# Value products in six-unit blocks, three banks for first scores, and a new order of scores and maxima's transposes in a block-attention kernel

## The chip, the cores and the metric

The kernel runs on one core of one Trainium2 chip. Its time is device microseconds of that core; lower is better. The kernel before takes 678.67 us (median of 3 runs, 678.55 to 678.76). A core has TensorE (PE in the profile, with its weight loads as PEld), VectorE (DVE), ScalarE (ACT), GpSimd (POOL), and SyncE (SP), whose queue issues all DMAs here. [...]

## The reference

One transformer block with adaptive layer norms: sliding-window attention (16 heads of 28, window of 256 keys), then a dense layer with Mish. S = 2048 positions, D = 448, F = 1792.

```python
def _A_ref(x, wqkv, wo):
    H = 16; Dh = D // H; W = 256
    qkv = (x @ wqkv).reshape(B, S, 3, H, Dh).transpose(2, 0, 3, 1, 4)
    q, k, v = qkv[0], qkv[1], qkv[2]
    scores = jnp.einsum("bhqd,bhkd->bhqk", q, k) * (Dh ** -0.5)
    mask = (idx[:, None] - idx[None, :] >= 0) & (idx[:, None] - idx[None, :] < W)
    p = _softmax(jnp.where(mask, scores, -1e9))
    return einsum("bhqk,bhkd->bhqd", p, v).transpose(0, 2, 1, 3).reshape(B, S, D) @ wo

h = _layernorm(x) * (1 + ca) + sa
x = x + ga * _A_ref(h, A_wqkv, A_wo)
h = _layernorm(x) * (1 + cb) + sb
x = x + gb * (mish(h @ B_w1 + B_b1) @ B_w2)
```

(sa, ca, ga, sb, cb and gb are six rows of silu(c) @ w_mod.)

## The kernel before, in words

**Stages.** A start (to about 37 us) loads x and the weights and makes the first projections. Attention runs from there to about 376 us, with the projections of the next row group, the output projection of the last one and the loading of the dense layer's weights between its steps. Then the dense layer runs to the end, matmuls on `z` and `acc`.

**Tiling of attention.** The 2048 rows are four groups g of 512 (`GT`). A *slot* i is one head in one row group; there are 64 (`NS`), and four consecutive slots make a *quad* q of 12 units. For each slot the keys are those of its 512 rows and of the 256 before them, six tiles jj of 128. Their allowed pairs of (key tile, query tiles) are three blocks b of 512 columns (`BLOCKS`): 128 + 384, 256 + 256, and 384 + 128. In the first row group, whose keys begin with the group, the blocks have 384, 256 and 384 + 128 columns. A *unit* u is one block of one slot: `unit(u)` gives slot 4q + r % 4 and block r // 4, with r = u % 12. So units 0 to 3 of a quad are block 0 of its four heads, 4 to 7 block 1, 8 to 11 block 2.

**The steps.** The softmax needs each row's maximum ahead of its exponentials, so scores are computed twice:

- `A(i, t)` (first scores): one matmul of a query tile t with the 384 keys that it can see, into a PSUM bank `sA` (L687). VectorE adds the mask and takes the maximum over the keys into `mx` (L689, which appears as two rows, the reduction `junk` and the read of its accumulator). A quad's 16 first scores belong to the quad *after* the one that is being exponentiated. After the last score of a pair of slots, `M1` splits the 8 maxima into two parts `ms` on VectorE (L700, L701).
- `M2(pr)` transposes a pair's `ms` on TensorE (L705, `mt`), VectorE copies it to `mr` (L707), and a DMA writes it into two rows of the pair's query tile (`q<-mr`), so that the second scores come out with the maximum subtracted.
- `L(i)` loads a slot's queries and keys by two DMAs (`q<-scr`, `k<-scr`); `load_slot` calls it at r = 8, 11, 2 and 4.
- `B(u)` (second scores): the mask through small matmuls (L759) or through a copy by ScalarE (`seeds`, L739), then the score matmuls (L731) into one of two banks `sB`, then the exponential on ScalarE into `P` (L734), a ring of seven buffers.
- `PV(w)` (value products): for four units, the matmuls of `V` with `P` into the bank `pv` (L769), in fp32, which shows as two matmul rows each. Each head's 28 value columns and a column of ones are padded to 32, and head a of the quad writes partitions 32a to 32a + 31. A program matmul is made for each width and head, the narrower width first.
- `EV(q)` copies the finished bank to SBUF on ScalarE (L775), `E(q)` transposes it on TensorE in four pieces into a bank (L780, `et`), and `E2(q)` reads that bank on VectorE: the reciprocal of the sums (L788) and the scaling (L790, `on`).

**Order.** Every engine works its instructions off in program order. The loop over u writes them: a step of `pipe` (evacuations that lag behind their matmuls); then, where u - 5 is a multiple of 4, `PV` of the four units that are complete, and `EV` after a quad's third; then `B(u)`; then the first scores that are due at r; `M2` at r = 7 and r = 11; `load_slot`; `E` at r = 3 and `E2` at r = 4 for the quad before; then projections as `RATE[g]` allows (`step(g)`) and a step of the side work (`side_step`), which holds a VectorE piece back where two first scores are due; last the second score of this r. Score n of 16 is due at r = 1 + n * 10 // 16: two each at r = 1, 2, 4, 6, 7 and 9, one at 3, 5, 8 and 10.

**Banks of PSUM.** In attention: `sA` two, `sB` two, `mm` two (projections), `pv` one, and `tr` one, which `M2` and `E` share. A bank that is asked for again is waited for until its last reader has read it. In the last four slots (i >= 60) every other first score takes an `mm` bank. At the start `tr` also holds one of the three first projections (`first`).

Of the kernel before, what the change touches and what calls it, by code (L numbers as in the profile page):

```python
# [20 lines left out]
NQ, NK, NV = 8, 8, 10  # L21
# [30 lines left out]
def adaln_block(ctx: ExitStack, tc: tile.TileContext, x, wqkv, wo, w1, b1, w2, c, w_mod, out):  # L52
    nc = tc.nc
    PE, ACT, DVE, POOL = nc.tensor, nc.scalar, nc.vector, nc.gpsimd
# [3 lines left out]
    def dma(o, i):  # L58
        nc.sync.dma_start(o, i)
# [25 lines left out]
    def bank(tag, bufs, name):  # L85
        return PS[0].tile([128, 512], F32, name=name, tag=tag, bufs=bufs)
# [22 lines left out]
    two = wqkv[:, 128:1152].rearrange("r (a n) -> r a n", n=512)[:, :, 0:256]  # L109
# [41 lines left out]
    V = [(vp if j < 6 else vq).tile([128, H, 32], F32, name=f"v{j}") for j in range(NV)]  # L151
# [53 lines left out]
    def passes(xh, xl, wh, wl):  # L205
        r = []
        for ci in range(3):
            r += [(xh[:, ci], wh[:, ci]), (xh[:, ci], wl[:, ci]), (xl[:, ci], wh[:, ci])]
        return r + [(xh[:, 3], wh[:, 3]), (xl[:, 3], wh[:, 3])]
# [7 lines left out]
    def dup(x):  # L217
        POOL.tensor_copy(x[:, D:512], x[:, 384:448])
# [92 lines left out]
    def drain(*gs):  # L311
        for g in gs:
            for _ in g:
                pipe.step()
# [16 lines left out]
    def flush():  # L331
        while later:
            later.pop(0)()
# [45 lines left out]
    def qk_passes(g, m):  # L379
        ms = slice(QPOS[m], QPOS[m] + 128)  # L380
        return passes(*HT[g], wq3[:, :, ms], wql[:, :, ms])
# [56 lines left out]
    def wq_lo(part, ci, eng):  # L438
        c = slice(*QCOLS[part])
        split_lo(wqs[ci][:, c], wq3[:, ci, c], wql[:, min(ci, 2), c], ci, eng)  # L440
# [27 lines left out]
    sums(0, (2, 3), DVE)  # L468
    for t in range(4):
        dup(XS[0][t])  # L470
    pm = [bank("sA", 2, f"mc{h}") for h in range(2)]
    trs = [bank(*((f"sB{ci}", 1) if ci < 2 else ("mm", 2)), f"tr0{ci}") for ci in range(4)]
    hh, hl = HT[0] = [mid.tile([128, 4, GT], F32R, name=f"h{n}0", tag="on", bufs=2) for n in "hl"]
    warm = bank("pv", 1, "warm")
# [22 lines left out]
    for ci in (2, 3):  # L497
        wq_hi(0, ci)
        wq_lo(0, ci, POOL)
    first = [(m, bank(tag, b, f"qk0_{m}"), qk_passes(0, m)) for m, tag, b in ((0, "pv", 1), (3, "tr", 1), (4, "sA", 2))]  # L500
    def passes0(cs, half):
        for m, p, ps in first:
            for ci in cs:
                for n in range(3 * ci, min(3 * ci + 3, 11)):
                    if (n == 10 or n < 9 and n % 3 == 2) == half:
                        PE.matmul(p, ps[n][1], ps[n][0], start=(n == 0), stop=(n == 10))  # L506
# [159 lines left out]
    NS = NG * H  # L666
    NU = 3 * NS
    mx, Pt, pvb, et, O4 = {}, {}, {}, {}, {}
# [11 lines left out]
    def A(i, t):  # L680
        g, h = divmod(i, H)
        q, k = Q3[i % NQ], K3[i % NK]
        if i % 2 == 0 and t == 0:
            mx[i // 2] = att.tile([128, 2, 4], F32, name=f"mx{i}", tag="mx", bufs=2)
        c0 = max(256 - 128 * t, 0) if g == 0 else 0
        p = bank("mm" if i >= 60 and t % 2 else "sA", 2, f"sA{i}_{t}")
        PE.matmul(p[:, c0:384], q[0:84, t * 128:(t + 1) * 128], k[0:84, t * 128 + c0:t * 128 + 384],  # L687
                  start=True, stop=True)
        DVE.tensor_tensor_reduce(out=junk[:, c0:384], in0=p[:, c0:384], in1=mask[:, c0:384], scale=1.0,  # L689
                                 scalar=-3.0e38, op0=ALU.add, op1=ALU.max,  # L690
                                 accum_out=mx[i // 2][:, i % 2, t:t + 1])
        if i % 2 and t == 3:
            M1(i // 2)
# [3 lines left out]
    def M1(pr):  # L697
        m = ms[pr] = att.tile([128, 2, 8], F32R, name=f"ms{pr}", tag="ms", bufs=2)
        x = mx[pr].rearrange("p a t -> p (a t)")
        DVE.tensor_copy(m[:, 0], x)  # L700
        DVE.tensor_tensor(m[:, 1], x, m[:, 0].bitcast(F32), op=ALU.subtract)  # L701

    def M2(pr):
        p = bank("tr", 1, f"mt{pr}")
        PE.transpose(p[0:16, 0:128], ms[pr].rearrange("p i x -> p (i x)").bitcast(F32), ident)  # L705
        r = att.tile([16, 128], F32, name=f"mr{pr}", tag="mr", bufs=2)
        DVE.tensor_copy(r, p[0:16, 0:128])  # L707
        dma(Q2[pr % (NQ // 2)][84:86].bitcast(F32).rearrange("i a (t n) -> i (a t) n", t=4), r)

    def units(g, b):  # L710
        return [x for x in BLOCKS[b] if g > 0 or x[0] >= 2]

    def by_width(blocks):
        return sorted(blocks, key=lambda x: x[2] - x[1])
# [44 lines left out]
            PE.matmul(p[:, c:c + n], identr, strip[:, m:m + n], start=(i == 0), stop=False, skip_group_check=True)  # L759

    def PV(w):
        q, b = divmod(w, 3)
        g, h = divmod(4 * q, H)
        if b == 0:
            pvb[q] = bank("pv", 1, f"pv{q}")
        for n, (jj, t0, t1, c) in enumerate(by_width(units(g, b))):
            j = 4 * g - 2 + jj
            for a in range(4):
                PE.matmul(pvb[q][32 * a:32 * a + 32, t0 * 128:t1 * 128], V[j % NV][:, h + a, :],  # L769
                          Pt[4 * w + a][:, c:c + 128 * (t1 - t0)],  # L770
                          start=(b == 0 and n == 0), stop=False, skip_group_check=True)

    def EV(q):
        O4[q] = att.tile([128, GT], F32, name=f"o4_{q}", tag="o4")
        ACT.activation(O4[q], pvb[q], AF.Copy)  # L775

    def E(q):
        p = bank("tr", 1, f"et{q}")
        for t in range(4):
            PE.transpose(p[:, t * 128:(t + 1) * 128], O4[q][:, t * 128:(t + 1) * 128], ident)  # L780
        et[q] = p.rearrange("p (t a d) -> p t a d", t=4, a=4)
# [262 lines left out]
    def side_step(g, two):  # L1044
        i = g == NG - 1
        if not (told.get(i) == "bank" and pipe.held() or told.get(i) == "dve" and two):
            told[i] = next(side[i], None)
# [7 lines left out]
    def step(g):  # L1055
        return next(fillers[g], 99.0) or RATE[g]
# [13 lines left out]
    def load_slot(i):  # L1070
        if i >= NS:
            return
        g, h = divmod(i, H)
        f0, f1 = h * DH, D + h * DH
        need({f0 // 128, (f0 + 27) // 128, f1 // 128, (f1 + 27) // 128}, g)
        L(i)
# [29 lines left out]
            load_slot(4 + i)  # L1106
    later[:0] = late
    credit = 0.0
    for u in range(NU + 7):
        s, k = divmod(u, 3)  # L1110
        g = s // H
        if k == 0 and s % H == 0 and 0 < g < NG:
            drain(fillers[g - 1], *side[:g == NG - 1])
            flush()
        pipe.step()
        w, m = divmod(u - 5, 4)
        if m == 0 and 0 <= w < NU // 4:
            PV(w)
            if w % 3 == 2:
                EV(w // 3)  # L1120
        q, r = divmod(u, 12)
        if u < NU:
            B(u)
        tiles = [divmod(n, 4) for n in range(16) if 1 + n * 10 // 16 == r and 4 * q + 4 < NS]
        if r != 3:
            for a, t in tiles[:1]:
                A(4 * q + 4 + a, t)
        if r in (7, 11) and 4 * q + 4 < NS:
            M2(2 * q + 2 + (r == 11))
        for a in range(4):  # L1130
            if (u - (8, 11, 14, 16)[a]) % 12 == 0 and u >= (8, 11, 14, 16)[a]:
                load_slot(4 * ((u - (8, 11, 14, 16)[a]) // 12) + 8 + a)
        if r - 3 in (0, 1) and 0 <= (u - 12 - 3) // 12 < NS // 4:
            (E, E2)[r - 3](q - 1)
        if g < NG:
            v = u - 48 * g
            if v in (0, 2):
                chunk["v"] = 4 if v == 0 and g or 0 < g < NG - 1 else 2
            if v == 0:
                credit = 0.0  # L1140
            credit += RATE[g] * (2 if v < FRONT[g] else 1)
            while credit > 0.0:
                credit -= step(g)
            if r == 3:
                for a, t in tiles[:1]:
                    A(4 * q + 4 + a, t)
            if v > 1 and u > 10:
                side_step(g, len(tiles) > 1)
            if later and r in (1, 4, 5, 6, 8, 9) and u not in (4, 11, 12):
                later.pop(0)()  # L1150
        if u == NU:
            drain(fillers[NG - 1], side[1])
            while pipe.items:
                pipe.step()
            flush()
        if u - NU in TAIL:
            TAIL[u - NU]()
        for a, t in tiles[1:]:
            A(4 * q + 4 + a, t)
    for st in (FW["s2"], att_s, vp_s):  # L1160
        st.close()
    psa_s.close()
# [50 lines left out]
    for n in range(NN + 1):  # L1213
        g, f = divmod(n, NF)
# [43 lines left out]
```

## Time and profile before

| | before |
|---|---|
| Median of 3 runs | 678.67 us |
| Span of the profiled execution, first to last instruction | 674.8 us |
| Reductions of first scores, L689 | 256 rows junk, 135.7 us, mean 530 ns |
| First scores, L687 | 256 matmuls, 93.5 us, mean 370 ns |
| Value products, L769 | 704 matmul rows, 50.6 us, mean 402 ns |
| Second scores, L731 | 352 matmuls, 84.9 us, mean 316 ns |
| Exponentials, L734 | 192, 108.6 us, mean 571 ns |

A row of a timeline gives start, duration, engine, line, operation, the tile written and the tiles read, shapes and count; in brackets stands the idle time of the engine just ahead of it and what ended that. Matmul rows overlap, as a matmul begins while the one before it still drains, so the distance from start to start is what a matmul costs in a stream, not its duration. In a list of waits a row says who waited for whom, and then the total in us, the number of waits and the longest.

### The profile page before, as it was taken

What the parts mean: (1) busy time and instruction counts of PE and PEld (TensorE: products, weight loads), DVE (VectorE), ACT (ScalarE), POOL (GpSimd) and SP (SyncE); (2) the same over time, 40 slices, a digit from 0 to 9 for tenths busy, and PEclk for the clock granted to TensorE, in tenths of its full rate; (3) what the DMA queues carried; (4) which work ended last, traced back from release to release, by engine and by line L of the source; (5) the groups of instructions that cost most, each with busy time, mean ns of one, the idle gap of its engine ahead of it and who ended that gap; (6) DMA issues with size and microseconds to landing.
All of it is one profiled execution on the core that took longest, in us unless ns stands there. A gap on an engine that the chain in (4) does not pass through costs nothing.

```text
span 674.8 us, 10729 instructions
## 1 busy us (share of the span) xinstructions
PE 637.9 (95%) x3712; PEld 511.0 (76%) x3712; DVE 391.7 (58%) x1138; ACT 336.9 (50%) x584; POOL 120.9 (18%) x173
## 2 busy tenths in 40 slices
PE   4998999899999999998989999989999999999996
PEld 3876676577887678776666788878888888888885
DVE  6865676756677767567767333963485438631112
ACT  4554566678765677734667743442333323322221
POOL 6741010233011100000030245431012001100002
PEclk9999999999999999997999999999999999999999
DMA  8875775456855478434772654003000300010001
GB/s 227 225 234 191 263 260 159 134 149 197 279 138 156 140 220 289 144 107 113 192 217 63 220 162 137 14 1 110 0 1 0 109 2 0 1 54 1 1 0 54
DMA packets 49169, 83.77 MB, mean 124 GB/s; under 512 B 5838, under 2 KB 27612, under 8 KB 49116
## 3 DMA queue, kind: packets, MB, share of 16 engines
q1 hardware_dynamic: 49116, 83.10, 40.3%
q8 instruction: 29, 0.48, 0.3%
q14 instruction: 24, 0.20, 0.1%
HBM read 53.45 MB, written 29.36 MB: 123 GB/s over the span
## 4 chain that ended last, share of the span: by engine, by line
PE 66%; DVE 15%; issue 12%; DMA 3%; ACT 2%; POOL 1%; SPq 0%; POOLq 0%; DVEq 0%; ACTq 0%
PE z L970 15%; PE qk L321 8%; DVE junk L689 6%; PE sA L687 6%; PE pv L769 6%; PE sB L731 5%; PE acc L1179 4%; PE acc L1178 4%; PE acc L1177 4%; PE wo L321 3%; PE qk_v L321 3%; DVE yt L897 3%; PE sB L759 2%; DMA k<-scr 1%; PE qk L506 1%
## 5 line engine op out<-in xcount | busy, mean ns | idle before, releaser
L689 DVE CUSTOM_DVE_ANT_0 junk<-sA,strip 128x384 bf16<-128x384 f32 (+2 forms) x256 | 135.7, 530 | 91.6 <-PE sA L687 76.7
L734 ACT ACTIVATE P<-sB 128x512 f32<-128x512 f32 (+2 forms) x192 | 108.6, 571 | 99.1 <-PE sB L731 96.7
L978 DVE TENSOR_TENSOR al<-t,ah 128x512 fp32r<-128x512 f32 x56 | 41.2, 736 | 137.2 <-ACT ah L977 136.8
L976 ACT ACTIVATE t<-z,b1c 128x512 f32<-128x512 f32 x56 | 38.4, 686 | 156.8 <-PE z L970 145.8
L687 PE MATMUL sA<-k,q 84*128 84x384 f32 (+2 forms) x256 | 93.5, 370 | 10.7 <-DVE mx L689 6.2
L970 PE MATMUL z<-hhf,w 128*128 128x512 f32 x224 | 89.0, 397 | 0.0
L970 PE MATMUL z<-hlf,w 128*128 128x512 f32 x224 | 88.8, 396 | 0.0
L731 PE MATMUL sB<-q,k 86*128 86x384 f32 (+1 forms) x352 | 84.9, 316 | 0.0
L1179 PE MATMUL acc<-w2h,al 128*128 128x448 f32 x224 | 82.1, 366 | 1.9 <-DVE al L978 1.9
L1177 PE MATMUL acc<-w2h,ah 128*128 128x448 f32 x224 | 81.9, 366 | 0.0
L1178 PE MATMUL acc<-w2l,ah 128*128 128x448 f32 x224 | 81.8, 365 | 0.0
L731 PEld LDWEIGHTS sB<-q,k 86*128 86x128 f32 x352 | 59.4, 193 | 13.1 <-issue 5.1
L970 PE MATMUL z<-hhf,w1l 128*128 128x512 f32 x168 | 66.5, 396 | 0.0
L687 PEld LDWEIGHTS sA<-k,q 84*128 84x128 f32 x256 | 48.3, 191 | 23.2 <-DVE mx L689 15.1
L897 DVE STREAM_TRANSPOSE yt<-xn 32x128 f32<-32x128 f32 x192 | 58.1, 302 | 2.6
L739 ACT ACTIVATE sB<-strip 128x512 f32<-128x512 bf16 (+2 forms) x95 | 54.6, 575 | 3.0
L769 PE MATMUL pv<-P,v 128*32 128x256 f32 (+2 forms) x704 | 50.6, 402 | 0.0
L970 PEld LDWEIGHTS z<-hlf,w 128*128 128x128 f32 x224 | 42.1, 188 | 10.1
L970 PEld LDWEIGHTS z<-hhf,w 128*128 128x128 f32 x224 | 42.1, 188 | 9.1 <-issue 0.6
L1179 PEld LDWEIGHTS acc<-w2h,al 128*128 128x128 f32 x224 | 42.1, 188 | 5.9 <-DVE al L978 2.6
L1177 PEld LDWEIGHTS acc<-w2h,ah 128*128 128x128 f32 x224 | 42.1, 188 | 5.0
L1178 PEld LDWEIGHTS acc<-w2l,ah 128*128 128x128 f32 x224 | 42.1, 188 | 4.8
(155 smaller groups left out, 1024.2 us busy)
## 6 DMA issues: line engine op xcount, KB each, us to landing
k<-scr SPq DMA_DIRECT2D x48, 252.0 KB
q<-scr SPq DMA_DIRECT2D x64, 168.0 KB
scr<-st SPq DMA_DIRECT2D x21, 512.0 KB
scr<-st SPq DMA_DIRECT2D x29, 256.0 KB
x<-x1d SPq DMA_DIRECT2D x10, 448.0 KB
xin<-in_A_x_dram SPq DMA_DIRECT2D x8, 448.0 KB
xr<-in_A_x_dram SPq DMA_DIRECT2D x16, 224.0 KB
x1d<-xr SPq DMA_DIRECT2D x16, 224.0 KB
```

The source lines that it names most:

```text
L321: PE.matmul(p, b, a, start=(n == 0), stop=(n == 10))
L687: PE.matmul(p[:, c0:384], q[0:84, t * 128:(t + 1) * 128], k[0:84, t * 128 + c0:t * 128 + 384], start=True, stop=True)
L689: DVE.tensor_tensor_reduce(out=junk[:, c0:384], in0=p[:, c0:384], in1=mask[:, c0:384], scale=1.0, scalar=-3.0e38, op0=ALU.add, op1=ALU.max ...
L731: PE.matmul(p[:, c:c + 128 * (t1 - t0)], k[:, jj * 128:(jj + 1) * 128], q[:, t0 * 128:t1 * 128], start=False, stop=True, skip_group_check= ...
L734: ACT.activation(P[:, c0:], p[:, c0:], AF.Exp, scale=SCALE)
L739: ACT.activation(p[:, c0:], strip[:, c + c0:c + 512], AF.Copy)
L769: PE.matmul(pvb[q][32 * a:32 * a + 32, t0 * 128:t1 * 128], V[j % NV][:, h + a, :], Pt[4 * w + a][:, c:c + 128 * (t1 - t0)], start=(b == 0 ...
L897: DVE.transpose(y4[32 * j:32 * j + 32, ci, :, 32 * i:32 * i + 32], x4[32 * i:32 * i + 32, :, ci, 32 * j:32 * j + 32])
L970: PE.matmul(zb[n], ps[m][1], ps[m][0], start=(m == 0), stop=(m == 10))
L1177: PE.matmul(p, ah[n][:, ts], w2h[f], start=(f == 0), stop=False)
L1178: PE.matmul(p, ah[n][:, ts], w2l[f], start=False, stop=False)
L1179: PE.matmul(p, al[n][:, ts], w2h[f], start=False, stop=(f == NF - 1))
```

## The change

- **PV in blocks of six units.** `PV(w)` now runs where u - 7 is a multiple of 6, twice in a quad, at r = 7 and at r = 1 of the next quad. The first takes block 0 of all four heads and block 1 of heads 0 and 1, the second block 1 of heads 2 and 3 and block 2 of all four. `EV` follows the second.
- **Banks.** `tr` is gone. `sA` has three banks, which serve all first scores (also those of the last four slots) and `M2`; `E` takes the bank `pv`. At the start, one of the first projections moves from `tr` to `sA`.
- **Order in a quad.** A table `scores` gives each first score a place (r, slot). The slots of an iteration are: 0 ahead of `B`, 1 right behind it, 2 behind `E`/`E2`, 3 behind the first step of projections, 4 behind all of them, 5 at the end. Three scores (7, 8, 9) stand at r = 6, none at r = 5, 11 and 0. `M2` of the first pair moves to slot 0 of r = 7, behind that block of `PV` and ahead of `B`, that of the second pair from behind `B` at r = 11 to slot 4 there, behind `load_slot` and the projections. `side_step` goes by the new table.

```diff
-    pm = [bank("sA", 2, f"mc{h}") for h in range(2)]
+    pm = [bank("sA", 3, f"mc{h}") for h in range(2)]
...
-    first = [(m, bank(tag, b, f"qk0_{m}"), qk_passes(0, m)) for m, tag, b in ((0, "pv", 1), (3, "tr", 1), (4, "sA", 2))]
+    first = [(m, bank(tag, b, f"qk0_{m}"), qk_passes(0, m)) for m, tag, b in ((0, "pv", 1), (3, "sA", 3), (4, "sA", 3))]
...
-        p = bank("mm" if i >= 60 and t % 2 else "sA", 2, f"sA{i}_{t}")
+        p = bank("sA", 3, f"sA{i}_{t}")
...
     def M2(pr):
-        p = bank("tr", 1, f"mt{pr}")
+        p = bank("sA", 3, f"mt{pr}")
...
     def PV(w):
-        q, b = divmod(w, 3)
+        q, e = divmod(w, 2)
         g, h = divmod(4 * q, H)
-        if b == 0:
+        if e == 0:
             pvb[q] = bank("pv", 1, f"pv{q}")
-        for n, (jj, t0, t1, c) in enumerate(by_width(units(g, b))):
-            j = 4 * g - 2 + jj
-            for a in range(4):
-                PE.matmul(pvb[q][32 * a:32 * a + 32, t0 * 128:t1 * 128], V[j % NV][:, h + a, :],
-                          Pt[4 * w + a][:, c:c + 128 * (t1 - t0)],
-                          start=(b == 0 and n == 0), stop=False, skip_group_check=True)
+        for b, heads in (((0, (0, 1, 2, 3)), (1, (0, 1))), ((1, (2, 3)), (2, (0, 1, 2, 3))))[e]:
+            for n, (jj, t0, t1, c) in enumerate(by_width(units(g, b))):
+                j = 4 * g - 2 + jj
+                for a in heads:
+                    PE.matmul(pvb[q][32 * a:32 * a + 32, t0 * 128:t1 * 128], V[j % NV][:, h + a, :],
+                              Pt[12 * q + 4 * b + a][:, c:c + 128 * (t1 - t0)],
+                              start=(b == 0 and n == 0), stop=False, skip_group_check=True)
...
     def E(q):
-        p = bank("tr", 1, f"et{q}")
+        p = bank("pv", 1, f"et{q}")
...
+    scores = {(1, 0): [0], (1, 3): [1], (2, 0): [2], (3, 0): [3, 4], (4, 1): [5], (4, 5): [6], (6, 1): [7, 8, 9], (7, 1): [10], (7, 3): [11], (8, 1): [12], (9, 1): [13], (9, 5): [14], (10, 1): [15]}
+    M2_AT = {(7, 0): 0, (11, 4): 1}
+
+    def place(q, r, slot):
+        if 4 * q + 4 >= NS:
+            return
+        for n in scores.get((r, slot), ()):
+            A(4 * q + 4 + n // 4, n % 4)
+        if (r, slot) in M2_AT:
+            M2(2 * q + 2 + M2_AT[r, slot])
...
-        w, m = divmod(u - 5, 4)
-        if m == 0 and 0 <= w < NU // 4:
+        w, m = divmod(u - 7, 6)
+        if m == 0 and 0 <= w < NU // 6:
             PV(w)
-            if w % 3 == 2:
-                EV(w // 3)
+            if w % 2:
+                EV(w // 2)
         q, r = divmod(u, 12)
+        place(q, r, 0)
         if u < NU:
             B(u)
-        tiles = [divmod(n, 4) for n in range(16) if 1 + n * 10 // 16 == r and 4 * q + 4 < NS]
-        if r != 3:
-            for a, t in tiles[:1]:
-                A(4 * q + 4 + a, t)
-        if r in (7, 11) and 4 * q + 4 < NS:
-            M2(2 * q + 2 + (r == 11))
+        two = 4 * q + 4 < NS and sum(len(scores.get((r, x), ())) for x in range(6)) > 1
+        place(q, r, 1)
         for a in range(4):
             if (u - (8, 11, 14, 16)[a]) % 12 == 0 and u >= (8, 11, 14, 16)[a]:
                 load_slot(4 * ((u - (8, 11, 14, 16)[a]) // 12) + 8 + a)
-        if r - 3 in (0, 1) and 0 <= (u - 12 - 3) // 12 < NS // 4:
-            (E, E2)[r - 3](q - 1)
+        if r in (3, 4) and 0 <= (u - 12 - 3) // 12 < NS // 4:
+            (E, E2)[r > 3](q - 1)
+        place(q, r, 2)
...
+            n = 0
             while credit > 0.0:
                 credit -= step(g)
-            if r == 3:
-                for a, t in tiles[:1]:
-                    A(4 * q + 4 + a, t)
+                n += 1
+                if n == 1:
+                    place(q, r, 3)
+            if n == 0:
+                place(q, r, 3)
+            place(q, r, 4)
             if v > 1 and u > 10:
-                side_step(g, len(tiles) > 1)
+                side_step(g, two)
...
-        for a, t in tiles[1:]:
-            A(4 * q + 4 + a, t)
+        place(q, r, 5)
```

## The prediction

> **What bounds the kernel now.** I read the page first, then the chain of work that ended last, then the waits of the weight loads, then busy time by quad, then single blocks in the timeline.
>
> ```profile
> span 674.8 us, 10729 instructions
> PE 637.9 (95%) x3712; PEld 511.0 (76%) x3712; DVE 391.7 (58%) x1138; ACT 336.9 (50%) x584; POOL 120.9 (18%) x173
> PE 66%; DVE 15%; issue 12%; DMA 3%; ACT 2%; POOL 1%; SPq 0%; POOLq 0%; DVEq 0%; ACTq 0%
> ```
>
> TensorE is busy for 95% of the span and makes up 66% of the chain; VectorE is the only other engine with a large share of it (15%). The change lies between 37 and 376 us, where attention runs beside projections; what follows there (matmuls on z and acc) is left as it is, and starts when attention ends, so a microsecond won or lost in attention is taken as one at the end. The profiled span stands 3.9 us under the median of the runs (678.67); I make the sum against the span and carry those 3.9 us over unchanged.
>
> Attention runs in 16 quads of heads, 12 units each. Busy time in four of them (columns: PE, PEld, DVE, ACT, POOL busy with counts, granted clock, DMA share, GB/s):
>
> ```profile
> 108.70:124.80 16.10, 13.56 (x92) 8.28 (x91) 11.65 (x43) 9.13 (x20) 0.00 (x0) 1.00 0.59 159
> 168.20:190.80 22.60, 22.60 (x160) 18.43 (x162) 14.84 (x50) 16.85 (x32) 0.63 (x2) 1.00 0.68 223
> 302.30:324.60 22.30, 19.64 (x140) 14.04 (x141) 14.40 (x47) 10.31 (x19) 0.40 (x1) 0.85 0.42 121
> 343.50:361.70 18.20, 15.49 (x125) 9.97 (x128) 12.94 (x48) 11.57 (x21) 4.41 (x9) 0.91 0.47 143
> ```
>
> The second is the usual kind: PE has no idle time at all, and whatever is added to PE there is paid. The other three have few projections to fill in, and PE idles 2.54, 2.66 and 2.71 us. What it waits for, first over 57 to 362 us, then in those three (waited for: us in total, times, longest):
>
> ```profile
> PEld sA L687 <- DVE mx L689: 14.3, 32, 1.6
> PEld mt L705 <- DVE ms L701: 7.7, 13, 1.5
> ...
> PEld sA L687 <- DVE mx L689: 3.9, 9, 0.5
> PEld mt L705 <- DVE ms L701: 1.2, 1, 1.2
> ...
> PEld sA L687 <- DVE mx L689: 3.1, 4, 1.6
> PEld mt L705 <- DVE ms L701: 0.6, 1, 0.6
> ...
> PEld mt L705 <- DVE ms L701: 2.0, 2, 1.5
> PEld sA L687 <- DVE mx L689: 0.3, 1, 0.3
> ```
>
> So first scores waiting for a bank, and the maxima's transposes waiting for the maxima, cost at most 14.3 + 7.7 = 22.0 us. The three quads hold 3.9 + 1.2 + 3.1 + 0.6 + 2.0 + 0.3 = 11.1 of it, the rest 10.9.
>
> **Value products: the price.** PE runs them with 32 output columns to a head, four heads abreast on four column groups. Three blocks, each with its successor, one with the two matmuls ahead of it, and a plain fp32 product on the whole array:
>
> ```profile
> 59.23 0.85 PE L769 MATMUL pv<-P,v 128*32 128x384 f32 x8
> 60.02 0.23 PE L759 MATMUL sB<-strip,identr 128*128 128x128 bf16 x1
> ...
> 64.77 0.39 PE L321 MATMUL qk<-hl,wq 128*128 128x512 f32 x1
> 65.00 0.40 PE L321 MATMUL qk<-hh,wq 128*128 128x512 f32 x1
> 65.33 0.64 PE L769 MATMUL pv<-P,v 128*32 128x256 f32 x8
> 65.90 0.34 PE L759 MATMUL sB<-strip,identr 128*128 128x128 bf16 x2
> ...
> 154.14 1.07 PE L769 MATMUL pv<-P,v 128*32 128x128 f32 x16
> 155.14 0.51 PE L731 MATMUL sB<-q,k 86*128 86x256 f32 x2
> ...
> 134.00 0.92 PE L577 MATMUL ga<-wm,ones 112*128 112x448 f32 x2
> 134.75 0.27 PE L759 MATMUL sB<-strip,identr 128*128 128x256 bf16 x1
> ```
>
> From start to successor, 256 columns a head take 0.57 us, 384 take 0.79, and 512 (eight rows of 128 and eight of 384) take 1.00: about 0.213 us per 128 columns and 0.147 fixed. Ahead of the block the gap is 0.33 instead of 0.23, so 0.10 more. A block costs **0.25 us** beside its columns; what its end does to the next weight load I leave out. The change makes 32 blocks of 48: 16 x 0.25 = **4.0 us saved**.
>
> Against that stands how the six units fall on the column groups. The first block of a quad holds block 0 for four heads (512 columns) and block 1 for heads 0 and 1 alone (512 more on two groups); the second holds block 1 for heads 2 and 3, and block 2 for four. Groups 2 and 3 have nothing to do in the one half step, groups 0 and 1 nothing in the other. The busiest group streams 1024 columns per block, 2048 per quad, where it was 3 x 512 = 1536. That is 512 x 0.213 / 128 = 0.853 us per quad in the 12 quads from the second row group on, and 256 columns (0.427) in the first four, whose blocks have 384, 256 and 512: 10.24 + 1.71 = **11.95 us added**. Two groups abreast occur nowhere in the trace. Lower bound: they stream twice as fast, and nothing is added. Upper: 11.95. I take the upper, as the nearest row speaks for it: the ga product, one stream on the whole array, needs 0.75 us for two passes of 448, or 0.107 per pass and 128 columns, just what each of four streams needs (0.213 for two). So they share no port that two could have to themselves. Net: 11.95 - 4.0 = **+7.95 us**.
>
> [...]
>
> **Waits: what the third bank and the order take away.** Two reductions in a stretch where VectorE has no rest:
>
> ```profile
> 112.77 0.56 DVE L689 CUSTOM_DVE_ANT_0 junk<-sA,strip 128x384 bf16<-128x384 f32 x1 [0.51 <-PE sA L687]
> 113.48 0.56 DVE L689 CUSTOM_DVE_ANT_0 junk<-sA,strip 128x384 bf16<-128x384 f32 x1
> ```
>
> They follow each other by 0.71 us. With a third bank a score waits for the reduction three back, not two, so an isolated wait of up to 0.71 us is gone; the mean one is 14.3 / 32 = 0.45. Three scores (7, 8, 9) now stand ahead of the block at r = 7, which feeds VectorE for 2.1 us while PE is away for 1.85. The first transpose of a quad then comes behind that block, the second behind a unit's projections. Outside the three quads I take 80% of 10.9, **8.7 us**; the fifth is for waits that only move. Inside them VectorE has 16 x 0.71 = 11.4 us of reductions alone, nearly all of it between r = 1 and r = 10, and a deeper queue wins about one period for each saturated stretch: a third of 11.1, **3.7 us**. Together 12.4; the bounds are 0 and 22.0.
>
> **Moved steps and new waits.** The second transpose takes its copy and its q<-mr DMA along, past the loads of the slot at r = 11 on SP's queue, which no longer stand behind it:
>
> ```profile
> 124.06 0.28 PE L705 MATMUL mt<-ident,ms 128*16 128x128 f32 x1 [0.96 <-DVE ms L701]
> 124.82 0.62 SPq L59 DMA_DIRECT2D q<-mr  x1
> 127.38 0.34 PE L759 MATMUL sB<-strip,identr 128*128 128x128 bf16 x2
> ```
>
> Its data is needed by the scores at r = 2, here 2.6 us after the issue, without a recorded wait. It comes later by the projections of r = 11 (some 0.5 to 1 us), and the block at r = 1 grows by up to 0.85, which gives most of it back: I take nothing; without that cover, up to 1 us in 16 quads, bounded above by the wait going back into the sum. The output transposes (et) move into the pv bank: they already wait for ACT's copy of that bank, but the block at r = 7 now waits for VectorE's last read of et, with all of PE's queue behind it. The latest such read is in the quad from 343.5:
>
> ```profile
> 351.76 0.62 DVE L790 TENSOR_TENSOR on<-et,rc 128x448 f32<-128x448 f32 x1
> 353.04 0.28 PE L759 MATMUL sB<-strip,identr 128*128 128x256 bf16 x1
> ```
>
> It ends at 352.38, and the scores of r = 7 start at 353.04: 0.66 us to spare, so nothing, or some tenths where VectorE is in arrears. The maxima's transpose takes a place in the sA ring until mr is copied; that, and the last four heads' loss of the mm banks, is part of the fifth above. ACT's P ring of seven is now full at each block, but unit u's exponential stands behind PE's scores of u, which stand behind the block: no new wait. The third first projection moving from tr to sA at the start: nothing, as the bank is a fresh one.
>
> Sum: +7.95 - 8.7 - 3.7 = **-4.45 us**; span 670.3, time 678.67 - 4.45 = **674.2**.
>
> **Rivals.** (a) *The half-empty steps win*: slower as soon as less than 7.95 of the 22.0 us is recovered (36%). For it: most quads are like that of 168.2, with nothing to recover, and in the three others VectorE sets the pace. With 4.5 recovered: 678.67 + 3.4 = 682.1. Chance 0.23. (b) *The ring is no deeper than it was*, because the transpose sits in it and VectorE in arrears holds all three banks; only the transposes' 7.7 goes: +0.25, 678.9. The short mean wait speaks against it. Chance 0.15. (c) *All 22.0 go*: -14.05, 664.6. Against it: VectorE's own load in three quads. The clock could add to this: in two quads it is granted at 0.85 and 0.91, which is 0.15 x 22.3 + 0.09 x 18.2 = 5.0 us at most, to 659.6. It fell near this row:
>
> ```profile
> 305.98 0.44 PE L687 MATMUL sA<-k,q 84*128 84x384 f32 x1 [1.36 <-DVE mx L689]
> ```
>
> [...] Chance of (c) 0.13. (d) *Two groups stream at double rate*: -4.0 - 12.4 = -16.4, 662.3. The ga row speaks against it. Chance 0.06.
>
> **How the numbers follow.** The forecast has the remaining 0.43. Faster by over 0.2% (1.36 us, about what a measurement of this kernel can tell from no change): 0.43 + 0.13 + 0.06 = 0.62; within: 0.15; slower: 0.23. The range reaches to (a) and to (c) without the clock: 664.5 to 682.5, leaving out (d), the clock's part of (c) and a tail of (a), some 0.18.
>
> **What the profile after would show.** Blocks of pv, 32 of them, with about 1.85 us to the successor from the second row group on (half step full price), or about 1.0 if (d). Waits of sA for mx and of mt for ms: near 10 us together if I am right, over 14 if (a) or (b). The quad that was 22.6 us long with PE full should be a little longer; those at 232 and 254 about even. I would be wrong above all if waits moved from sA to sB, pv or VectorE's other readers, or if the block at r = 7 waited for et.

## The result, and the profile after

The changed kernel takes 673.3 us (median of 10 runs, 669.04 to 678.0) beside 678.16 us (median of 10) for the kernel before: a ratio of 0.9943, 95% interval 0.9918 to 0.9968. The ratio is estimated from all runs and is not the quotient of the two medians, which is 0.9928; the same holds for the ratios below. So the change makes the kernel faster, by 0.57%, where 0.66% was forecast. The span of the profiled execution is 672.4 us.

The page of the changed kernel, in the rows that answer to those shown of before:

```profile
span 672.4 us, 10728 instructions
PE 642.2 (96%) x3712; PEld 520.1 (77%) x3712; DVE 394.3 (59%) x1138; ACT 336.4 (50%) x584; POOL 120.8 (18%) x173
PE 75%; issue 11%; DVE 9%; ACT 2%; DMA 2%; POOL 1%; POOLq 0%; SPq 0%; DVEq 0%; ACTq 0%
```

PE is busy for 4.3 us more in a span that is 2.4 us shorter, so it idles 30.2 us instead of 36.9, and its share of the chain grows from 66% to 75% while VectorE's falls from 15% to 9%: the chain now passes through PE where it used to wait for VectorE. What was bought is waits; what was paid is PE work. The work first, three of the new blocks with their successors in the timeline (24, 12 and 20 matmul rows):

```profile
189.91 1.92 PE L770 MATMUL pv<-P,v 128*32 128x256 f32 x24
191.76 0.44 PE L687 MATMUL sA<-k,q 84*128 84x384 f32 x1
...
64.70 1.27 PE L770 MATMUL pv<-P,v 128*32 128x384 f32 x12
65.91 0.28 PE L705 MATMUL mt<-ident,ms 128*16 128x128 f32 x1
...
109.22 1.49 PE L770 MATMUL pv<-P,v 128*32 128x256 f32 x20
110.63 0.44 PE L687 MATMUL sA<-k,q 84*128 84x384 f32 x1
```

From start to start: 1.85, 1.21 and 1.41 us. For 1024, 640 and 768 columns on the busiest column group the sum 0.147 + 0.213 per 128 gives 1.85, 1.21 and 1.43. In these blocks a half step therefore streamed on two column groups at just the rate that four have, 0.213 us per 128 columns.

Now the waits over 57 to 362 us, of the weight loads and, below, of the matmuls themselves:

```profile
PEld mt L705 <- DVE ms L701: 5.9, 8, 1.9
PEld sA L687 <- DVE mx L689: 4.5, 8, 1.1
PEld mt L705 <- DVE mx L689: 3.7, 8, 0.8
...
PE mt L705 <- DVE ms L701: 3.4, 2, 1.7
PE sA L687 <- DVE mx L689: 2.4, 4, 0.9
```

The scores' waits for a bank have gone from 14.3 to 4.5 us. Read from the weight loads alone, the transposes wait longer than before (5.9 + 3.7, against 7.7). But the idle time of PEld was no loss where a matmul still streamed: the first transpose of a quad stands behind a long block, and in the middle row above (64.70 to 65.91) its start comes 1.21 us after the block's, which is the block's own length and nothing more. The matmuls' own waits for ms are 3.4 us in two places (before the transposes at 125.35 and 355.28 us). In the kernel before, the same view had:

```profile
PE sA L687 <- DVE mx L689: 5.9, 20, 1.4
PE mt L705 <- DVE ms L701: 4.9, 10, 1.3
PE sA L687 <- DMA k<-scr: 2.0, 2, 1.1
```

### The profile page after: what moved, and what is told of

Read it like the earlier page. It is cut to its first block, busy times and chain, and to the rows that moved or that the text cites. A ratio compares the mean times of both kernels' runs of the same rounds, so it can differ in the third digit from the quotient of the medians.

```text
span 672.4 us, 10728 instructions
## 1 busy us (share of the span) xinstructions
PE 642.2 (96%) x3712; PEld 520.1 (77%) x3712; DVE 394.3 (59%) x1138; ACT 336.4 (50%) x584; POOL 120.8 (18%) x173
## 4 chain that ended last, share of the span: by engine, by line
PE 75%; issue 11%; DVE 9%; ACT 2%; DMA 2%; POOL 1%; POOLq 0%; SPq 0%; DVEq 0%; ACTq 0%
PE z L971 15%; PE qk L321 9%; PE pv L770 9%; PE sA L687 6%; PE sB L731 6%; PE wo L321 5%; PE acc L1191 4%; PE acc L1189 4%; PE acc L1190 4%; PE qk_v L321 4%; DVE yt L898 3%; DVE junk L689 2%; PE sB L759 2%; PE qk L506 1%; PE mt L705 1%
## 5 line engine op out<-in xcount | busy, mean ns | idle before, releaser
L687 PE MATMUL sA<-k,q 84*128 84x384 f32 (+2 forms) x256 | 82.3, 359 | 3.2 <-DVE mx L689 2.4
L770 PE MATMUL pv<-P,v 128*32 128x128 f32 (+2 forms) x704 | 61.0, 409 | 0.0
L687 PEld LDWEIGHTS sA<-k,q 84*128 84x128 f32 x256 | 46.9, 193 | 17.9 <-issue 8.7
```

## The experiments

Twelve kernels; ratios are to the kernel before. They take the change apart along its four parts: the length of the blocks of value products, the banks, the order of the first scores, and the places of the maxima's transposes.

| | blocks | banks | scores | transposes | ratio (95%) |
|---|---|---|---|---|---|
| changed kernel | six | new | new | new | 0.9943 (0.9918 to 0.9968) |
| 1 | four, late | new | new | new | 0.9872 (0.984 to 0.9903) |
| 2 | six | old | old | old | 1.0126 (1.0097 to 1.0156) |
| 3 | four, late | new | old | old | 1.0003 (0.9976 to 1.003) |
| 4 | four | old | new | new | 1.0055 (1.0033 to 1.0077) |
| 5 | eight and four | new | another | later | 1.0072 (1.0047 to 1.0098) |
| 6 | four, late | new | old | new | 0.991 (0.9883 to 0.9937) |
| 7 | four, late | new | new | old | 1.006 (1.0035 to 1.0086) |
| 8 | four | new | new | new | 1.0223 (1.019 to 1.0256) |
| 9 | four, late | new | new | second: behind the loads | 0.9868 (0.9825 to 0.9911) |
| 10 | four, late | new | new | first: old | 0.9915 (0.9887 to 0.9942) |
| 11 | eight and four | new | new | first: later | 0.9955 (0.9925 to 0.9985) |
| 12 | four | old | old | new | 0.9952 (0.9927 to 0.9978) |

"Late" blocks of four stand at r = 7, 10 and 1, the plain ones at 5, 9 and 1 as before. Late blocks with the old banks were not run, so the effect of the new banks is always that of banks and late blocks together.

**1. Blocks of four in the changed kernel.** `PV` of the kernel before, with

```diff
-        w, m = divmod(u - 7, 6)
-        if m == 0 and 0 <= w < NU // 6:
-            PV(w)
-            if w % 2:
-                EV(w // 2)
+        w, m = divmod(u - 7, 12)
+        if m in (0, 3, 6) and 0 <= w < NS // 4:
+            PV(3 * w + m // 3)
+            if m == 6:
+                EV(w)
```

> The changed kernel with value products back in blocks of four units (three a quad, at r = 7, 10 and 1, so that each still comes behind the reads of et); banks and order of scores as changed. Theory A (half-empty steps cost 12 x 0.85 + 4 x 0.43 us and fewer blocks save 16 x 0.25, net near +7 us): this kernel is some 7 us faster than the changed one, ratio to before near 0.984, blocks of 1.00 us, 48 of them. Theory B (the long blocks are what lets VectorE catch up, so they pay for themselves): as the changed kernel or slower, ratio 0.994 or above, with waits of sA for mx clearly over the changed kernel's 4.5 us.

668.63 us (666.52 to 672.48), ratio 0.9872. It beats both kernels, as theory A has it: the rest of the change is worth 1.28% (8.7 us of 678), and the six-unit blocks give back 0.71% (4.8 us) of it. By the two intervals that can be some 2 to 7.5 us, so the 7 us expected are not excluded. If it is less, a reason would be that in the changed kernel part of the longer block runs while VectorE works off scores for which PE would otherwise wait. The two profiles agree with that, without proving it: with the six-unit blocks PE is busy 8.9 us longer (642.2 against 633.3) but idles 2.9 us less (30.2 against 33.1), at a mean granted clock of 0.986 against 0.991.

**2. Six-unit blocks alone**, in the kernel before: the new `PV`, and in the loop

```diff
-        w, m = divmod(u - 5, 4)
-        if m == 0 and 0 <= w < NU // 4:
+        w, m = divmod(u - 7, 6)
+        if m == 0 and 0 <= w < NU // 6:
...
```

> The kernel before with the six-unit blocks of value products alone; two banks for first scores and the old order. Theory A: slower than before by 5 to 8 us, ratio near 1.010, as the waits of sA and mt stay near 22 us. Theory B: faster than before, ratio near 0.996, with waits of sA for mx falling from 14.3 us by several us.

685.96 us, ratio 1.0126: slower by 8.5 us (0.0126 of 678), near the forecast's 7.95. Waits of sA for mx, 12.2 us, fell by 2.1 only. Theory B falls.

**3 and 4. Banks alone, order alone.** Experiment 3 is the kernel before with the late blocks of four and

```diff
-        p = bank("mm" if i >= 60 and t % 2 else "sA", 2, f"sA{i}_{t}")
+        p = bank("sA", 3, f"sA{i}_{t}")
-        p = bank("tr", 1, f"mt{pr}")
+        p = bank("sA", 3, f"mt{pr}")
-        p = bank("tr", 1, f"et{q}")
+        p = bank("pv", 1, f"et{q}")
```

(and the two banks at the start). Experiment 4 is the changed kernel with these lines undone, and with `PV` and its places of the kernel before; so its "order" is that of the scores and of the transposes.

> The kernel before with the banks alone (three for first scores, the maxima's transposes among them, et in pv), old order of scores, blocks of four at r = 7, 10 and 1. Theory A with the third bank as the main cause: waits of sA for mx fall from 14.3 us to 6 or less, ratio near 0.987. Rival (the order of the scores is the cause, the third bank only holds more of the same): waits of sA stay above 10 us, ratio 0.997 to 1.003.

> The kernel before with the new order of first scores and of the maxima's transposes alone: two banks, blocks of four at r = 5, 9 and 1. If the third bank is the main cause: three scores in a row have two banks, so waits of sA stay above 12 us, ratio 0.997 to 1.008. If the order is the cause: waits of sA fall below 8 us, ratio near 0.988. For the transposes' waits (7.7 us before): if the move of M2 helps by itself they fall below 4 us here.

Neither is worth anything alone: 1.0003 and 1.0055. With the order alone, three scores in a row meet two banks and wait longer (first row below, weight loads in experiment 4: 22.0 us, where the kernel before has 14.3). With the banks alone, the scores wait less for mx but now for other things (PE's own waits in experiment 3):

```profile
PEld sA L687 <- DVE mx L689: 22.0, 34, 1.6
...
PE sA L687 <- DMA k<-scr: 4.9, 4, 1.6
PE sA L687 <- DVE mx L689: 2.1, 4, 1.0
PE sA L687 <- DVE ms L700: 1.6, 1, 1.6
```

Experiment 3 misses the expectation that the third bank is the main cause, and its rival as well, whose ratio came but not its waits (4.9 us of sA for mx by the weight loads, not over 10). Experiment 4 comes out as expected if the third bank is the main cause (waits of sA over 12 us, ratio 0.997 to 1.008), while the transposes' waits fell only to 5.3 us, not below 4. So neither part is the cause by itself. My next theory was that the transposes, which sit in the scores' ring and take an order of their own on VectorE and SP, were what undid the third bank.

**6, 7 and 12. The transposes' places.** Experiment 6 is 3 with `M2` moved to its new places, 7 is 1 with `M2` at the old ones, 12 is the kernel before with `M2` moved and nothing else:

```diff
-        if r in (7, 11) and 4 * q + 4 < NS:
-            M2(2 * q + 2 + (r == 11))
...
+        if r == 7 and 4 * q + 4 < NS:
+            M2(2 * q + 2)
         if u < NU:
             B(u)
...
+            if r == 11 and 4 * q + 4 < NS:
+                M2(2 * q + 3)
             if v > 1 and u > 10:
```

(6 and 12.) In 7: `M2_AT = {(7, 1): 0, (11, 1): 1}`.

> The third experiment (banks alone, ratio 1.000) with the maxima's transposes at their new places, scores in the old order. If the transposes in the ring were what undid the third bank: ratio near 0.990, gaps ahead of sA well below the third experiment's 14.6 us. If the order of the scores is what the third bank needs: ratio 0.996 to 1.001.

> The first experiment (blocks of four, ratio 0.987) with the maxima's transposes at their old places: behind score 10 at r = 7 and behind B at r = 11. If the transposes' place is the key: ratio 0.995 or above, waits for ms back near 8 us. If the scores' order is: ratio near 0.989, only the second transposes wait, some 3 us more.

> The kernel before with the two transposes alone at the new places (ahead of B at r = 7; behind load_slot and the projections at r = 11); two banks for first scores, tr, blocks at r = 5, 9 and 1, old order of scores. If the transposes' places are worth what they seem (0.009 between the third and the sixth experiment) on any banks: ratio 0.989 to 0.993. If they count only with the third bank, where the transpose sits in the scores' ring: ratio 0.997 to 1.002, with waits of sA for mx still near 14 us.

Ratios 0.991, 1.006 and 0.9952. Moving two instructions per quad is worth 0.9% on the new banks (3 to 6), 1.9% with the new order as well (7 to 1), and 0.5% by itself, between the two ranges of its expectation. In 7 the ratio is as expected if the places are the key, but not the reason: the waits for ms are 3.1 us by the weight loads, not near 8. The profile of 7 says where the time went; PE's own waits, in 7 and then in 10 (first transpose old, second new):

```profile
PE sA L687 <- DMA k<-scr: 11.0, 8, 2.7
PE sA L687 <- DVE mx L689: 3.0, 7, 1.0
...
PE sA L687 <- DVE mx L689: 3.3, 7, 0.9
PE mt L705 <- DVE ms L701: 1.8, 2, 1.2
PE sA L687 <- DMA k<-scr: 1.7, 2, 1.1
```

Scores wait for *loads*. SP's queue is why; the second transpose of one quad in 7 (VectorE's copy, then SP's queue) and, below the second dots, the same quad in 1:

```profile
112.83 0.28 DVE L707 COPY mr<-mt 16x128 f32<-16x128 f32 x1
...
113.13 0.62 SPq L59 DMA_DIRECT2D q<-mr  x1
113.85 0.36 SPq L59 DMA_DIRECT2D q<-scr  x1
114.27 0.38 SPq L59 DMA_DIRECT2D k<-scr  x1
...
104.74 0.31 SPq L59 DMA_DIRECT2D q<-scr  x1
105.10 0.38 SPq L59 DMA_DIRECT2D k<-scr  x1
109.70 0.62 SPq L59 DMA_DIRECT2D q<-mr  x1
```

In 7 the slot's loads of r = 11 stand behind the DMA of the maxima, which is issued when `mr` is written (112.83 + 0.28 = 113.11); in 1 they went out 4.6 us ahead of it.

**9 and 10. Which transpose, and which queue.** `M2_AT` is `{(7, 0): 0, (11, 2): 1}` in 9 (the second right behind `load_slot`, still ahead of the projections) and `{(7, 1): 0, (11, 4): 1}` in 10.

> The first experiment (blocks of four, ratio 0.987) with the second pair's transpose directly behind load_slot at r = 11, so ahead of the projections. With both transposes at their old places the ratio was 1.006, and PE waited 11.0 us for k<-scr. If the cause is SP's queue (loads behind a q<-mr that waits for mr): with the loads ahead of it the waits for k<-scr stay under 2 us, and the ratio is 0.987 to 0.990, only the waits for ms grow by some 2 us. If it is the place ahead of the projections itself: ratio 0.993 or above, with waits for ms of 6 us or more.

> The first experiment with the first pair's transpose alone at its old place, behind score 10 at r = 7, so that its mr copy stands behind the reductions of 7 to 10. If the first pair's place counts (its q<-mr stands ahead of the loads at r = 8): ratio 0.993 or above, waits for k<-scr over 5 us. If the second pair's place is the whole cause: ratio 0.986 to 0.990.

9 stays at 0.9868, with 1.2 us of PE's waits for k<-scr and 2.4 for ms: standing ahead of the projections shows no cost; standing ahead of the loads, as in 7, does (11.0 us of waits for k<-scr). From 7 to 10, which moves the second transpose alone, the ratio falls from 1.006 to 0.9915. The first transpose's place may be worth the remaining 0.4% (0.9915 against 0.9872), but those intervals overlap, and its waits for k<-scr did not grow as the expectation had it; that part stays open.

These runs also show what each part is worth when it alone is taken back out of experiment 1: banks and late blocks 1.8% (experiment 4, 1.0055), the transposes' places 1.9% (experiment 7, 1.006), the order of the scores 0.4% (experiment 6, 0.991). The intervals of the last pair overlap, so the new order of scores is not shown to be worth anything.

**8. Blocks of four at their old places**, r = 5, 9 and 1, otherwise as experiment 1:

```diff
-        w, m = divmod(u - 7, 12)
-        if m in (0, 3, 6) and 0 <= w < NS // 4:
+        w, m = divmod(u - 5, 4)
+        if m == 0 and 0 <= w < NU // 4:
...
```

> The first experiment with its blocks of four at r = 5, 9 and 1, as in the kernel before, so that a quad's first block stands one iteration behind the reads of et in the same bank. If the reads of et hold PE up there: slower than 0.987 by several us, ratio near 0.995, with waits of pv for VectorE's on (L791) in the list. If they are done in time: ratio 0.985 to 0.989.

692.71 us, ratio 1.0223, the slowest of all; the expectation had the wait, but only some 0.8% for it, not 3.5%. PE's waits have a row that no other kernel has:

```profile
PE pv L769 <- DVE on L790: 13.6, 12, 1.8
PE mt L705 <- DVE ms L701: 6.3, 8, 1.8
```

The block at r = 5 needs the bank in which VectorE still reads et, and all of PE's queue stands behind it. Two units later (experiment 1) the row is gone. The row holds 13.6 of the 24 us between the two kernels, and the transposes' waits 4.2 more (6.3 against 2.1); the rest was not taken apart. So the banks of the change need a first block later than r = 5; r = 7 is late enough, r = 6 was not tried.

**5 and 11. Two blocks without a half-empty step.** Blocks 0 and 1 of all four heads at r = 9, block 2 at r = 1; P in a ring of nine, mr and rc in one buffer each. Against the changed kernel:

```diff
-        for b, heads in (((0, (0, 1, 2, 3)), (1, (0, 1))), ((1, (2, 3)), (2, (0, 1, 2, 3))))[e]:
+        for b in ((0, 1), (2,))[e]:
...
-        w, m = divmod(u - 7, 6)
-        if m == 0 and 0 <= w < NU // 6:
+        w, m = divmod(u - 9, 12)
+        if m in (0, 4) and 0 <= w < NS // 4:
...
```

`M2_AT` has the first transpose at (8, 0) in 5, and at (9, 0) in 11; 5 has scores 9, 10 and 11 at (8, 1) instead of 7, 8 and 9 at (6, 1).

> The changed kernel with value products in two blocks a quad as well, but of eight units (blocks 0 and 1 of four heads, at r = 9) and four (block 2, at r = 1), so that no step is half empty; P in a ring of nine, mr and rc in one buffer instead of two, scores 9 to 11 ahead of the long block. Theory A (the half-empty steps are the price, the fewer blocks a saving of 0.25 us each): blocks of 1.85 and 1.00 us, 4 us faster than the first experiment (blocks of four, 0.987), ratio near 0.981. Theory B (a long block costs by its length, as ScalarE and VectorE run dry during it): no faster than 0.987, with more waits of sB for ScalarE.

> Blocks of eight units at r = 9 and four at r = 1, as in the fifth experiment, but with the changed kernel's order of scores; the first transpose behind the long block at r = 9. The fifth had 13.8 us of PEld waits of mt for ms and a ratio of 1.007. If its order was what lost: waits for ms below 6 us, ratio 0.981 to 0.986, below the first experiment's 0.987 by the 16 x 0.25 us of the blocks saved. If blocks of eight lose by themselves: ratio 0.99 or above.

Ratios 1.0072 and 0.9955. Experiment 5 had an order of its own, and its transposes wait for ms: 13.8 us by the weight loads, 7.7 by PE itself, where experiment 1 has 2.1. With the changed kernel's order 11 is better, but not the 0.981 to 0.986 of the expectation, though its blocks cost what they should (1.86 and 1.00 us to the successor). Weight loads' waits of sA for mx, 11 and then 1:

```profile
PEld sA L687 <- DVE mx L689: 10.7, 19, 1.4
...
PEld sA L687 <- DVE mx L689: 5.8, 10, 1.1
```

The 16 x 0.25 us of blocks saved do not show. PE idles 4.7 us more than in experiment 1 (37.8 against 33.1), which is about as much again; that this comes from the long block standing at another place than the burst of scores is argued, not shown, as the P ring and the buffers of mr and rc differ too, and the mean granted clock of the profiled runs was 0.982 against 0.991. No order made for this block was tried beyond that of experiment 5.

## Why the prediction was right

The sign, the size and the range hold. Two of its terms were too large, by some 3 and 4 us and with opposite signs, so that the sum came as near as it did is partly luck; and the loads behind q<-mr, which the transposes' places decide, had no term.

- **Blocks.** +7.95 us was right as a price: the blocks last 1.85, 1.21 and 1.41 us as worked out, and alone they cost 8.5 us (experiment 2). In the changed kernel they cost 4.8 (0.9943 - 0.9872 = 0.71%; 2 to 7.5 us by the intervals). So taking them in full everywhere was probably too simple: where PE waits for VectorE, a longer block may have covered part of a wait, which no run shows by itself. Rival (d), twice the rate on two groups, is refuted by the blocks' lengths (1.85 us, where it had about 1.0).
- **Waits.** I took 12.4 us of 22.0 as recovered. Everything but the six-unit blocks is worth 8.7 us (experiment 1). The weight loads' waits, from which the 22.0 came, count too much: PE's own were 5.9 + 4.9 = 10.8 us in the same stretch before, and 5.8 in the changed kernel. But PE's own count too little: from the kernel before to experiment 1 the profiled span falls by 8.4 us, PE's idle time only by 3.8 (36.9 to 33.1), and the rest is busy time of the same matmuls (637.9 to 633.3), which was not taken apart. My range had room for that; the sum came out near because the blocks' cost was too large as well.
- **The cause.** I explained the recovered waits by the third bank first. Alone with late blocks it is worth nothing (experiment 3), and the order of scores and transposes alone costs 0.55% (experiment 4). Banks, order and transposes' places are worth 1.28% together. Without the places the other two lose (1.006, experiment 7), and without the banks and late blocks the other two lose as well (1.0055, experiment 4); without the new order of scores a gain of 0.9% is left (experiment 6).
- **SP's queue.** The prediction saw that the loads no longer stand behind q<-mr, and took nothing for it. With the new banks and order this is what keeps the scores fed: 11.0 us of waits for k<-scr without it, 1.7 with it, and 1.4% of the time (7 and 10). Against the kernel before, which had only 2.0 us of such waits, the term is smaller: the places alone are worth 0.5% (experiment 12), waits for mx and ms among it. Why the loads come too late in 7 and not in the kernel before, where they stand behind q<-mr as well (issued at 107.78 and 108.50 us), was not taken further apart.
- **et in the bank of pv.** "0.66 us to spare" at r = 7 was right, as the changed kernel has no wait of pv for VectorE; at r = 5 it costs 3.5% (experiment 8 against 1).
- **What the profile would show.** Waits of sA for mx and of mt for ms near 10 us: by the weight loads 10.4 (4.5 + 5.9), or 14.1 with the transposes' waits that stand under mx, which is the value I had given to the rivals; by PE itself 5.8. Another 2.0 us of PE's own waits are now those of sB for ScalarE, of which the kernel before shows none. The quad that was full went from 22.60 to 22.1 us by the stretch chosen (167.8 to 189.9 in the profile after), but from 21.95 to 22.08 us when taken from its block at r = 1 to that of the next quad (168.77 to 190.72 before, 167.83 to 189.91 after). That sign depends on where the quad is cut and decides nothing.

## What to carry to other kernels

The order on PE was here also an order in SP's queue: in experiment 1 a slot's loads went out 4.6 us ahead of the DMA of the maxima, in 7 they stood behind it, and the second transpose's place alone took the waits for k<-scr from 11.0 to 1.7 us (7 to 10). So ask of each moved step which loads stand behind its DMA, not only who waits for its data. The small matmuls abreast paid for the busiest column group: the blocks of 1024, 640 and 768 columns on that group took 1.85, 1.21 and 1.41 us, so a step that filled half of the groups cost a full one. A long block may be cheaper where another engine is behind (4.8 us for the six-unit blocks in the changed kernel, 8.5 alone), which the profiles here suggest but do not prove. And judge a bundle of edits by its parts in combination: here banks and order were worth nothing or less alone, the banks (with late blocks) 1.8% together with the transposes' places and the order, and the part that cost most (the six-unit blocks) could be undone, for a kernel at 0.9872.

## What the runs showed of the hardware

The granted clock halved for some microseconds here and there, not all at the same places in each kernel: it was 0.50 over 308 to 312 us in the profile before, and over 54 to 58, 118 to 120 and 346 to 348 us in the profile after. The last two of these stretches, each below the 3 us ahead of it (columns as in the prediction):

```profile
115.00:118.00 3.00, 1.92 (x13) 0.97 (x14) 2.75 (x11) 1.55 (x4) 0.00 (x0) 0.87 0.92 222
...
118.00:120.00 2.00, 2.00 (x15) 0.67 (x8) 1.04 (x5) 0.00 (x0) 0.00 (x0) 0.50 0.04 14
...
343.00:346.00 3.00, 1.56 (x8) 0.84 (x7) 2.90 (x9) 2.13 (x4) 0.80 (x3) 0.99 0.95 267
...
346.00:348.00 2.00, 1.86 (x17) 1.06 (x19) 1.64 (x9) 0.00 (x0) 0.00 (x0) 0.50 0.39 128
```

Ahead of them PE was busy for 1.92 and 1.56 of 3 us, and its longest idle times there were 0.77 and 0.86 us: here half the clock followed on stretches in which PE was only thinned out. A block of products that fell into the first of these stretches took nearly twice its time: the twelve-row block at 117.19 us has its successor after 2.28 us, at a granted clock of 0.51, where the same block of an earlier quad, at 64.70 us and a clock of 1.00, takes 1.21. The spread between runs goes with the clock: of the changed kernel's ten, the two with a mean granted clock of 0.997 took 669.04 and 670.02 us, that with 0.981 took 678.0. What sets these stretches off was not tested, nor how much of the differences between the kernels is clock.
